# Keys and values of an attention kernel from unsplit fp32 products, two token blocks side by side

## The chip, the cores and the metric

The kernel runs on one core of one Trainium2 chip, in one launch. The metric is the device time of that core in microseconds (us), lower is better; the time of a kernel is the median of its runs. In the tables of the profile PE is the matrix engine (TensorE), PEld its weight loads, DVE the vector engine, ACT the scalar engine, POOL the GpSimd engine, and SP the engine whose queue issues all of this kernel's DMAs.

## The reference

Two independent blocks are computed and joined on the last axis. The first is attention with one key/value head, the second a two-dimensional Fourier mixing.

```python
q = (x @ wq)  # 2048 x 1024 tokens, 32 heads of 32
k = x @ wk    # 2048 x 32, shared by all heads
v = x @ wv    # 2048 x 32
p = softmax(q k^T * 32 ** -0.5)
a = (p @ v, heads joined) @ wo
b = dft_seq_re @ (xb @ dft_hid_re.T) - dft_seq_im @ (xb @ dft_hid_im.T)
out = concatenate([a, b], axis=-1)
```

## The kernel before, in words

**Split products.** All large products are made of three: each operand is rounded to `float32r` (the high part, `rh` or `mh`) and the rounding error is kept (the low part, `rl` or `ml`), and a product is high by high, low by high and high by low. A chunk of 128 of the contracted axis is thus three PE products of 512 columns (`product`, line 345). A `Group` (line 77) is one tile of 128 x 512 outputs with its chunks, 24 products for 8 chunks. Its right side is moving data in tiles of 128 x 512, its left side two tiles of four weight chunks. What a group does with its result is its `post`.

**Filling.** The groups stand in one list, and `take(n)` (line 351) issues the next n products of that list; `pos["fill"]` counts them. `pump` (line 290) runs ahead of that count: two lines (`RL` for right sides, `ML` for left sides, lines 256 and 257) load, convert to a high part and convert to a low part so many products before the need. While `pos["fill"]` is under `START`, ACT makes the high parts and DVE the low ones; later POOL makes both (`cast`, line 173, and `lo`, line 243). All DMAs go through SP in program order, and a DMA whose buffer isn't free holds up all that stand behind it.

**The start.** The tokens are four blocks of 512 (`b` = 0 to 3), each 8 chunks of `xT`. In the list stand first four key/value groups (`kv_group`, line 415: x chunks against the joined `wkv` of 64 columns, so that only 64 of 128 output rows are in use), for blocks 1, 2, 3 and 0 in that order of loading, then two query groups of block 0; `START` is these six groups, 144 products. `kv_post` (line 393) copies keys and values out, puts high, high and low parts of the keys into rows 0 to 95 of `kst` (one written by DVE, two moved by DMA), and transposes the values into `v` by four PE transposes, 20 products later. The first 26 tiles of x are loaded at once into buffers that are needed later for other things (line 718 on: `pp`, name `p`, and `hp`, names `h0` to `h7`). After the first six groups `open_unit(0)` (line 585) loads the scaled queries of the first unit, which a query group's post has stored to DRAM in a high part `qh` and a low part `ql`, into `qst`. Then come 66 more products of query groups.

**Units.** A unit is four heads of one query block, 32 units in all. `score_step` (line 699) makes the scores of one tile, `DVE` takes the row maximum, `ACT` the exponential with its row sum. 44 score steps run ahead, each with `take(7)`. In the main loop (line 752) one step is a score step, an `expo` (two products and an exponential of 128 x 1024 on ACT), every eighth step a `pv` (16 plain fp32 products of 32 output columns, four of them side by side in the array), and as many products of the list as `goal` (line 741) spreads evenly over 1024 steps. The logarithms of a unit's row sums, tile `mt`, go into `qst` by DMA in `lse_4` (line 646), four steps before the first `expo` of the unit. The list after the query groups is the Fourier part and then the output product; the last groups are written out by hand (line 768 on), and each copies its result through a tile of the pool `op` (line 131) to the output.

**Pools that the change touches.** `op` holds the staging tiles of results: two of `qh`, one of `ql` (line 425). `yp` (line 130) holds six tiles `y0`, `qsp` three tiles `qst`, `onp` one `ov`.

Of the kernel before, what the change touches and what calls it, by code (L numbers as in the profile page):

```python
# [8 lines left out]
F32 = mybir.dt.float32  # L9
F32R = mybir.dt.float32r  # L10
AF = mybir.ActivationFunctionType
# [5 lines left out]
P = 128  # L17
# [3 lines left out]
DH = 32  # L21
W = 512
NG = 8
NQ = 4
NC = 16
ND = D // P
# [61 lines left out]
def tile_kernel(ctx: ExitStack, tc, xT, wq, wkv, wo, xbT, wT, cT, out):  # L88
    nc = tc.nc
    te = Ordered(tc, nc.tensor)  # L90
    act = Ordered(tc, nc.scalar)
    dve = Ordered(tc, nc.vector)
    gp = Ordered(tc, nc.gpsimd)
    sp = Ordered(tc, nc.sync)
    scale = float(DH) ** -0.5

    def pool(stack, name, bufs, **kw):
        kw.setdefault("reuse_waits", "tile")
        return stack.enter_context(tc.tile_pool(name=name, bufs=bufs, **kw))
# [12 lines left out]
    keep = pool(ctx, "keep", 1)  # L112
    ident = keep.tile([P, P], F32, name="ident")
    make_identity(nc, ident)
    kst = keep.tile([P, S], F32R, name="kst")
    dve.memset(kst[96:P, :].bitcast(F32), 0.0)
    dve.memset(kst[96:98, :].bitcast(F32), 1.0)
    v = keep.tile([P, NC, DH], F32, name="v")

    ps_s = pool(ctx, "ps_s", 2, space=PSUM)  # L120
    ps_t = pool(ctx, "ps_t", 1, space=PSUM)
# [6 lines left out]
    rp = pool(ctx, "rp", NR, side="right")  # L128
    mp = pool(ctx, "mp", NM, side="right")
    yp = pool(ctx, "yp", NY, side="right")  # L130
    op = pool(ctx, "op", 2, side="right")
    hp = pool(ctx, "hp", 1, side="right")

    def move(q, to, of):
        q.dma_start(to.bitcast(F32), of.bitcast(F32))


    class Line:
# [32 lines left out]
    pos = {"fill": 0, "s": 0}  # L171
# [84 lines left out]
    RL = Line(NR0, NR, (40, 40, 14, 8), load_r, comb, hi_r, lo)  # L256
    ML = Line(NM0, NM, (52, 36, 27, 21), load_m, comb, hi_m, lo)
# [87 lines left out]
    def product(g, ps, j):  # L345
        c, w = divmod(j, 3)
        l, r = g.left[c // 4], g.right[c]
        a = (l.lo if w == 2 else l.hi)[:, c % 4]
        te.matmul(ps[:g.rows], a, r.lo if w == 1 else r.hi, start=j == 0, stop=j == g.n - 1)

    def take(n):
        for _ in range(n):
            if cur["group"] >= len(groups):
                return
            g = groups[cur["group"]]
            j = pos["fill"] - g.at
            if j == 0:
                cur["ps"] = bank("psb", True)
            if j % 3 == 0:
                RL.force(g.right[j // 3])  # L360
            if j % 12 == 0:
                ML.force(g.left[j // 12])
            product(g, cur["ps"], j)
            pos["fill"] += 1
            if j == g.n - 1:
                cur["group"] += 1
                assert all(hasattr(it, "done") for it in g.ys)
                g.post(cur["ps"])
                cur["at"] += 1
                used[cur["bank"]] = cur["at"]  # L370
                cur["bank"] = None
                if g.ys:
                    at(pos["fill"] + 2 * BEHIND, lambda n=len(g.ys): yused.__setitem__(0, yused[0] + n))
            pump()
            run_later()
# [14 lines left out]
    def x_set(b):  # L390
        return [Item([(lambda c=c: xT[b, c], 1)]) for c in range(ND)]

    def kv_post(b):
        cols = slice(b * W, (b + 1) * W)

        def post(ps):
            kv = yp.tile([P, W], F32, name="y0")[:2 * DH]
            act.activation(kv, ps[:2 * DH], AF.Copy)
            dve.tensor_copy(kst[0:DH, cols], kv[0:DH])
            kl = yp.tile([P, W], F32, name="y0")[:DH].bitcast(F32R)  # L400
            dve.tensor_sub(kl, kv[0:DH], kst[0:DH, cols].bitcast(F32))
            move(sp, kst[DH:2 * DH, cols], kst[0:DH, cols])
            move(sp, kst[2 * DH:3 * DH, cols], kl)

            def v_out():
                pv = ps_s.tile([P, 2 * W], F32, name="pss")[:, :W].rearrange("p (a b) -> p a b", a=4)
                for j in range(4):
                    te.transpose(pv[:, j, :2 * DH], kv[:, j * P:(j + 1) * P], ident[:2 * DH, :2 * DH])
                dve.tensor_copy(v[:, b * 4:(b + 1) * 4, :], pv[:, :, DH:2 * DH])
            at(pos["fill"] + 20, v_out)  # L410
        return post

    wkv_items = [Item([(lambda q=q: wkv[:, q * 4:(q + 1) * 4, :], 1)]) for q in range(2)]

    def kv_group(b, xs):
        return Group(wkv_items, xs, kv_post(b), rows=2 * DH)

    ready = set()

    def q_group(b, g, xs):  # L420
        left = [Item([(lambda q=q: wq[g, :, q * 4:(q + 1) * 4, :], 1)]) for q in range(2)]

        def post(ps):
            qh = op.tile([P, W], F32R, name="qh")
            ql = op.tile([P, W], F32R, name="ql", bufs=1)
            if pos["fill"] <= START:
                act.activation(qh, ps, AF.Copy, scale=scale)
            else:
                dve.tensor_scalar_mul(qh, ps, scale)
            dve.scalar_tensor_tensor(ql, ps, scale, qh.bitcast(F32), op0=ALU.mult, op1=ALU.subtract)  # L430
            store(qh_d[b][g], qh)
            store(ql_d[b][g], ql, ("q", b, g))
        return Group(left, xs, post)
# [123 lines left out]

    def x_groups(b, kv, q):  # L560
        xs = x_set(b)
        return ([kv_group(b, xs)] if kv else []) + ([q_group(b, g, xs) for g in range(NG)] if q else [])

    first = x_groups(0, True, True)
    start = x_groups(1, True, False) + x_groups(2, True, False) + x_groups(3, True, False) + first[:2]
    START = 24 * len(start)
    rest = first[2:] + x_groups(1, False, True) + x_groups(2, False, True) + x_groups(3, False, True)
    rest += list(stage1()) + list(stage2())
    w1, w0 = wo_set(1), wo_set(0)
    rest += [o_group(b, t, e, ws) for e, ws in ((1, w1), (0, w0)) for b in range(NQ - 1) for t in range(4)]  # L570
# [144 lines left out]
    TURN = 6  # L715
    LSE = {1: (lse_1,), 2: (lse_1b,), 4: (lse_2,), 8: (lse_4,)}

    room = [(lambda t=t, k=k: t[:, k]) for t in [pp.tile([P, 2, W], F32, name="p") for _ in range(9)] for k in range(2)]
    room += [(lambda t=t: t) for t in [hp.tile([P, W], F32, name=f"h{k}") for k in range(8)]]
    for n, (it, to) in enumerate(zip(RL.items, room)):  # L720
        it.t = [to()]
        sp.dma_start(it.t[0], it.srcs[0][0]())
        if n == 1:
            ML.pump()
    pump()
    take(START)
    open_unit(0)
    take(66)
    for s in range(SU + LEAD):
        score_step(s)  # L730
        take(7)
# [20 lines left out]
    for n in range(total):  # L752
        u, r = divmod(n, SU)
# [41 lines left out]
    for t, g in enumerate(last[4:]):  # L795
        ps = ps_b[t % 2].tile([P, W], F32, name="psb")
# [41 lines left out]
```

## Time and profile before

| | us |
|---|---|
| median of 3 runs (2790.85 to 2792.5) | 2790.86 |
| the profiled execution, whole | 2791.25 |
| its span in the profile | 2789.3 |
| PE busy in the span | 2763.8 |
| ACT busy | 2181.4 |
| POOL busy | 1651.0 |
| DVE busy | 1624.4 |

The profiled execution's own time is 1.95 us over its span, and 0.39 us over the median. A row of the timeline reads: start, duration, engine, line, operation, output <- inputs, shape, count, and in brackets the idle time of that engine ahead of the row with what ended it. Line 66 is that of a helper through which every instruction goes, so rows are told apart by the names of their tiles. A PE row of one product lasts longer than the step to the next product, because products overlap; the step from start to start is what counts. A plain fp32 product stands as two PE rows in the profile, a product of `float32r` parts as one.

### The profile page before, as it was taken

To read this page: it belongs to the slowest core of one execution; us is meant where nothing else is said; L and a number is where in the kernel's file an instruction comes from. 1 tells how busy PE (TensorE), PEld (TensorE's weight loads), DVE (VectorE), ACT (ScalarE), POOL (GpSimd) and SP (SyncE) were. 2 spreads that over 40 slices of the span, in tenths; PEclk is the share of its full clock that TensorE was granted. 3 is DMA by queue.
4 is the path that set the end of the run, shared out by engine and by line. 5 is a ranking of instruction groups with operands and counts; after the bars stand their busy time and mean duration, and the time that the engine had idled before them with its cause. 6 is when DMAs were issued, how large, how long until landed. Compare 5 with 4: busy or idle time off the path is not lost.

```text
span 2789.3 us, 40153 instructions
## 1 busy us (share of the span) xinstructions
PE 2763.8 (99%) x13904; PEld 1932.7 (69%) x13904; DVE 1624.4 (58%) x1864; ACT 2181.4 (78%) x3151; POOL 1651.0 (59%) x1622
## 2 busy tenths in 40 slices
PE   8999999999999999999999999999999999999999
PEld 5876767667666767666676767667676767676666
DVE  6766666666676665555555655555565555555411
ACT  4578888888788888888888888878888888888740
POOL 3755534665535538767686567798887885640110
PEclk9999999999999999999999999999999999999999
DMA  7544325766576554545453454555564552554455
GB/s 253 197 140 129 110 103 174 242 213 203 189 237 212 171 175 156 162 144 153 143 189 104 129 167 139 160 198 162 163 193 150 167 160 80 159 163 140 126 166 173
DMA packets 304203, 459.87 MB, mean 165 GB/s; under 512 B 32128, under 2 KB 97152, under 8 KB 304000
## 3 DMA queue, kind: packets, MB, share of 16 engines
q1 hardware_dynamic: 304000, 457.30, 51.6%
q8 instruction: 110, 1.80, 0.3%
q14 instruction: 93, 0.76, 0.1%
HBM read 351.54 MB, written 104.60 MB: 164 GB/s over the span
## 4 chain that ended last, share of the span: by engine, by line
PE 96%; DMA 1%; DVE 1%; ACT 1%; issue 0%; POOL 0%; SPq 0%; ACTq 0%; POOLq 0%; DVEq 0%
PE psb L66 61%; PE pss L66 18%; PE pst L66 17%; DMA p<-in_xT_dram 0%; DVE nm L66 0%; ACT pss L66 0%; SPq L66 0%; DVE rl L66 0%; ACT p L66 0%; DMA r<-s 0%; ACT rh L66 0%; DMA qst<-mt 0%; DMA ql<-ql 0%; DMA r<-in_xT_dram 0%; POOL ml L66 0%
## 5 line engine op out<-in xcount | busy, mean ns | idle before, releaser
L66 DVE TENSOR_REDUCE nm<-pss 128x1 f32<-128x1024 f32 x1024 | 1252.7, 1223 | 591.2 <-PE pss L66 590.3
L66 ACT ACTIVATE p<-pst 128x1024 f32<-128x1024 f32 x1024 | 1052.2, 1028 | 463.8 <-PE pst L66 461.3
L66 ACT ACTIVATE pss<-pss,nm 128x1024 f32<-128x1024 f32 x1024 | 1112.9, 1087 | 67.3 <-DVE nm L66 65.9
L66 PE MATMUL psb<-rh,mh 128*128 128x512 f32 (+1 forms) x1852 | 730.4, 394 | 9.7 <-ACT rh L66 8.3
L66 PE MATMUL psb<-rh,ml 128*128 128x512 f32 (+1 forms) x1852 | 730.1, 394 | 2.2 <-POOL ml L66 2.2
L66 PE MATMUL psb<-rl,mh 128*128 128x512 f32 (+1 forms) x1852 | 728.5, 393 | 0.3 <-DVE rl L66 0.3
L66 PE MATMUL pss<-kst,qst 128*128 128x512 f32 x2048 | 657.1, 402 | 1.3 <-ACT pss L66 1.2
L66 PE MATMUL pst<-qst,kst 128*128 128x512 f32 x2048 | 649.5, 398 | 4.4 <-DMA qst<-mt 3.6
L66 PEld LDWEIGHTS pss<-kst,qst 128*128 128x128 f32 x2048 | 372.2, 188 | 184.7 <-issue 102.3
L66 POOL TENSOR_TENSOR ml<-m,mh 128x512 fp32r<-128x512 f32 x340 | 438.8, 1291 | 48.2 <-ACT mh L66 40.4
L66 PE MATMUL psb<-p,v 128*32 128x512 f32 x4096 | 466.3, 596 | 0.0
L66 PEld LDWEIGHTS pst<-qst,kst 128*128 128x128 f32 x2048 | 377.4, 188 | 112.2 <-ACT p L66 20.8
L66 PEld LDWEIGHTS psb<-rh,mh 128*128 128x128 f32 (+1 forms) x1852 | 346.7, 187 | 95.9 <-ACT rh L66 9.0
L66 PEld LDWEIGHTS psb<-rh,ml 128*128 128x128 f32 (+1 forms) x1852 | 346.6, 187 | 86.7 <-POOL ml L66 3.5
L66 PEld LDWEIGHTS psb<-rl,mh 128*128 128x128 f32 (+1 forms) x1852 | 346.7, 187 | 84.5 <-DVE rl L66 1.4
L66 PEld LDWEIGHTS psb<-p,v 128*32 128x32 f32 x4096 | 120.0, 109 | 276.6 <-issue 265.6
L66 POOL CAST mh<-m 128x512 fp32r<-128x512 f32 x339 | 208.1, 614 | 166.0 <-PE psb L66 145.3
L66 POOL TENSOR_TENSOR r<-r,r 128x512 f32<-128x512 f32 x112 | 144.4, 1289 | 271.6 <-DMA r<-s 135.2
L66 POOL CAST rh<-r 128x512 fp32r<-128x512 f32 x214 | 131.5, 614 | 262.0 <-PE psb L66 144.9
L66 POOL TENSOR_TENSOR rl<-r,rh 128x512 fp32r<-128x512 f32 x214 | 276.2, 1291 | 3.9
L66 POOL TENSOR_TENSOR m<-m,m 128x512 f32<-128x512 f32 x192 | 247.9, 1291 | 28.7 <-DMA m<-in_xbT_dram 20.6
L66 DVE TENSOR_TENSOR ov<-ov,psb 128x512 f32<-128x512 f32 x96 | 66.0, 688 | 272.0 <-PE psb L66 272.0
(68 smaller groups left out, 929.5 us busy)
## 6 DMA issues: line engine op xcount, KB each, us to landing
m<-in_cT_dram SPq DMA_DIRECT2D x384, 256.0 KB, 3.7
r<-s SPq DMA_DIRECT2D x192, 256.0 KB, 4.3
y<-y SPq DMA_DIRECT2D x96, 256.0 KB, 4.6
r<-in_wT_dram SPq DMA_DIRECT2D x80, 256.0 KB, 3.7
m<-in_xbT_dram SPq DMA_DIRECT2D x80, 256.0 KB, 4.2
y<-u SPq DMA_DIRECT2D x80, 256.0 KB, 2.8
m<-in_wq_dram SPq DMA_DIRECT2D x64, 256.0 KB, 3.0
qst<-qh SPq DMA_DIRECT2D x64, 256.0 KB, 5.5
```

What stands on the lines that cost most here:

```text
L66: return lambda *a, **k: self.tc.keep_in_program_order(f(*a, **k))
```

## The change

Keys and values leave the list. `kv_pair` makes them for two blocks at once from x and `wkv` as they were loaded, in plain fp32: block one's 64 output rows in rows 0 to 63 of one PSUM tile, block two's in rows 64 to 127. It then splits the keys on DVE and moves all three parts by DMA. All 32 tiles of x are loaded at the start, the last six into two tiles of `qst`; those of blocks 0 and 1 are also what the query groups of these blocks convert, while blocks 2 and 3 are still loaded once more for their query groups later. Three products of zeros (the tile `v`, cleared first) are issued ahead of the first group. `START` falls from 144 to 48. The 66 products ahead of the first score become 24. Low parts of queries go into the ring `y0` of six, and `op` has three `qh`.

```diff
+    v = keep.tile([P, NC, DH], F32, name="v")
+    dve.memset(v, 0.0)
     dve.memset(kst[96:P, :].bitcast(F32), 0.0)
     dve.memset(kst[96:98, :].bitcast(F32), 1.0)
-    v = keep.tile([P, NC, DH], F32, name="v")
...
-    op = pool(ctx, "op", 2, side="right")
+    op = pool(ctx, "op", 3, side="right")
...
+    def kv_pair(blocks, xs):
+        ps = ps_s.tile([P, 2 * W], F32, name="pss")[:, :W]
+        for c in range(ND):
+            for n, x in enumerate(xs):
+                te.matmul(ps[n * 2 * DH:(n + 1) * 2 * DH], wkv_t[:, c * 2 * DH:(c + 1) * 2 * DH], x[c], start=c == 0, stop=c == ND - 1)
+        kv = yp.tile([P, W], F32, name="y0")
+        act.activation(kv, ps, AF.Copy)
+        kh = op.tile([P, W], F32R, name="qh")
+        dve.tensor_copy(kh, ps)
+        kl = yp.tile([P, W], F32, name="y0").bitcast(F32R)
+        dve.tensor_sub(kl, ps, kh.bitcast(F32))
+        for n, b in enumerate(blocks):
+            rows = slice(n * 2 * DH, n * 2 * DH + DH)
+            for r, part in enumerate((kh, kh, kl)):
+                move(sp, kst[r * DH:(r + 1) * DH, b * W:(b + 1) * W], part[rows])
+        def v_out():
+            pv = ps_t.tile([P, 2, W], F32, name="pst")[:, 0].rearrange("p (a b) -> p a b", a=4)
+            for j in range(4):
+                te.transpose(pv[:, j], kv[:, j * P:(j + 1) * P], ident)
+            for n, b in enumerate(blocks):
+                dve.tensor_copy(v[:, b * 4:(b + 1) * 4, :], pv[:, :, (2 * n + 1) * DH:(2 * n + 2) * DH])
+        at(pos["fill"] + 20, v_out)
...
-            ql = op.tile([P, W], F32R, name="ql", bufs=1)
+            ql = yp.tile([P, W], F32, name="y0").bitcast(F32R)
...
+    sets = [x_set(b) for b in range(NQ)]
+    start = [q_group(0, g, sets[0]) for g in range(2)]
...
+    zeros = v[:, :, :].rearrange("p a b -> p (a b)")
+    for _ in range(3):
+        te.matmul(ps_t.tile([P, 2, W], F32, name="pst")[:, 0], zeros[:, :P], zeros, start=True, stop=True)
...
+    load_x(0)
+    for it in sets[0]:
+        RL.force(it)
+    wkv_t = onp.tile([P, W], F32, name="ov")
+    sp.dma_start(wkv_t, wkv.rearrange("p a b -> p (a b)"))
+    load_x(1)
+    for it in start[1].left:
+        ML.force(it)
     pump()
-    take(START)
+    load_x(2)
+    load_x(3)
+    take(24)
+    kv_pair((0, 1), xs[:2])
+    take(24)
     open_unit(0)
-    take(66)
+    kv_pair((2, 3), xs[2:])
+    take(24)
```

What this makes of the order on two engines is shown at three places. In the rows, names carry the number of the buffer, and what stands in brackets is what the instruction waits for. First, the start of PE's row, before:

```order
L66 MATMUL psb_457<-rh_449,mh_417 64x512 [waits Activation_49]
L66 MATMUL psb_457<-rl_450,mh_417 64x512 [waits DVE_49]
L66 MATMUL psb_457<-rh_449,ml_418 64x512
L66 MATMUL psb_457<-rh_452,mh_417 64x512 [waits Activation_49]
L66 MATMUL psb_457<-rl_453,mh_417 64x512 [waits DVE_49]
L66 MATMUL psb_457<-rh_452,ml_418 64x512
```

and with the change, where `pst` is the PSUM tile of the zero products and `psb_512` that of the first query group:

```order
L66 MATMUL pst_395<-v_282 128x512 [waits DVE_49]
L66 MATMUL pst_397<-v_282 128x512 [waits PE_49]
L66 MATMUL pst_399<-v_282 128x512 [waits PE_49]
L66 MATMUL psb_512<-rh_440,mh_425 128x512 [waits Activation_49]
L66 MATMUL psb_512<-rl_441,mh_425 128x512 [waits DVE_49]
L66 MATMUL psb_512<-rh_440,ml_426 128x512
```

The first list product is now one of 128 output rows and of the queries, and each chunk of x still waits for ACT and then DVE to convert it. Second, PE at the passage from one group to the next. Before, from the second key/value group (`psb_559`) to the third (`psb_637`):

```order
L66 MATMUL psb_559<-rl_519,mh_420 64x512 [waits DVE_49]
L66 MATMUL psb_559<-rh_518,ml_421 64x512
L66 MATMUL psb_637<-rh_525,mh_417 64x512
L66 MATMUL psb_637<-rl_526,mh_417 64x512 [waits DVE_49]
L66 MATMUL psb_637<-rh_525,ml_418 64x512
```

With the change, from the first query group to the first pair; `p_401` to `p_408` are the tiles of x, two chunks each (401 to 404 block 0, 405 to 408 block 1), and `ov_472` holds `wkv`:

```order
L66 MATMUL psb_512<-rh_468,mh_428 128x512 [waits Activation_49]
L66 MATMUL psb_512<-rl_469,mh_428 128x512 [waits DVE_49]
L66 MATMUL psb_512<-rh_468,ml_429 128x512
L66 MATMUL pss_554<-p_401,ov_472 64x512 [waits DMAHW2_49,DMAHW0_49]
L66 MATMUL pss_554<-p_405,ov_472 64x512 [waits DMAHW3_49]
L66 MATMUL pss_554<-p_401,ov_472 64x512
L66 MATMUL pss_554<-p_405,ov_472 64x512 [waits DMAHW4_49]
L66 MATMUL pss_554<-p_402,ov_472 64x512
```

The pair alternates between the two blocks chunk by chunk, 16 products in all, and these wait for DMAs alone; before, every one of the 96 key/value products stood behind conversions. Third, SP between the loads of x and the first unit's queries, before:

```order
L66 DMA kst_281<-kst_281 32x512
L66 DMA kst_281<-y0_760 32x512
L66 DMA m0_774<-in_wq_dram 128x512
L66 DMA r0_792<-in_xT_dram 128x512
L66 DMA m0_797<-in_wq_dram 128x512
L66 DMA qh_0_0_57<-qh_813 128x512
L66 DMA ql_0_0_89<-ql_814 128x512
L66 DMA qst_819<-qh_0_0_57 32x4x512
L66 DMA qst_819<-ql_0_0_89 32x4x512
```

and with the change (`m0` are weights of queries, `qst_637` is the tile of the first unit, `qh_573` and `y0_575` are the keys' parts of blocks 0 and 1):

```order
L66 DMA kst_281<-qh_573 32x512 x2
L66 DMA kst_281<-y0_575 32x512
L66 DMA m0_593<-in_wq_dram 128x512
L66 DMA m0_615<-in_wq_dram 128x512
L66 DMA qh_0_1_58<-qh_631 128x512
L66 DMA ql_0_1_90<-y0_632 128x512
L66 DMA qst_637<-qh_0_0_57 32x4x512
L66 DMA qst_637<-ql_0_0_89 32x4x512
```

The loads of the first unit's `qst` now stand behind the stores of the second query group (`qh_0_1`, `ql_0_1`) too; before, only those of the first (`qh_0_0`, `ql_0_0`) stood ahead of them.

More of the change, by code (lines that the diff above doesn't have):

```diff
@@ L391, in x_set @@
         return [Item([(lambda c=c: xT[b, c], 1)]) for c in range(ND)]
[L393 to L411, printed above, removed]
@@ L413, in tile_kernel @@
-    wkv_items = [Item([(lambda q=q: wkv[:, q * 4:(q + 1) * 4, :], 1)]) for q in range(2)]
-    def kv_group(b, xs):
-        return Group(wkv_items, xs, kv_post(b), rows=2 * DH)
+    def kv_pair(blocks, xs):
[20 more added lines that the diff above has]
+        at(pos["fill"] + 20, v_out)
@@ L554, in o_group @@
         return Group([o_left(b, t, q) for q in range(2)], ws, post)
[L560 to L565, printed above, removed]
+    sets = [x_set(b) for b in range(NQ)]
+    start = [q_group(0, g, sets[0]) for g in range(2)]
     START = 24 * len(start)
-    rest = first[2:] + x_groups(1, False, True) + x_groups(2, False, True) + x_groups(3, False, True)
+    rest = [q_group(b, g, sets[b]) for b in range(NQ) for g in range(0 if b else 2, NG)]
     rest += list(stage1()) + list(stage2())
@@ L716, in tile_kernel, with load_x @@
     LSE = {1: (lse_1,), 2: (lse_1b,), 4: (lse_2,), 8: (lse_4,)}
[L718 to L724, printed above, removed]
-    pump()
-    take(START)
+    zeros = v[:, :, :].rearrange("p a b -> p (a b)")
+    for _ in range(3):
+        te.matmul(ps_t.tile([P, 2, W], F32, name="pst")[:, 0], zeros[:, :P], zeros, start=True, stop=True)
+    room = [t[:, k] for t in [pp.tile([P, 2, W], F32, name="p") for _ in range(9)] for k in range(2)]
+    room += [hp.tile([P, W], F32, name=f"h{k}") for k in range(8)]
+    room += [t[:, k].bitcast(F32) for t in [qsp.tile([P, 4, W], F32R, name="qst") for _ in range(2)] for k in range(4)]
+    xs = [[room[b * ND + c] for c in range(ND)] for b in range(NQ)]
+    def load_x(b):
+        for c in range(ND):
+            sp.dma_start(xs[b][c], xT[b, c])
+            if b < 2:
+                sets[b][c].t = [xs[b][c]]
+            if b == 0 and c == 0:
+                ML.pump()
+    load_x(0)
[6 more added lines that the diff above has]
+        ML.force(it)
+    pump()
+    load_x(2)
[3 more added lines that the diff above has]
+    take(24)
     open_unit(0)
-    take(66)
+    kv_pair((2, 3), xs[2:])
+    take(24)
     for s in range(SU + LEAD):
```

## The prediction, made before the change was run

> **What bounds the kernel now.** I read the engines' busy time first, then the chain that ended last, then the time by stage (columns: stretch, its length, then busy time and instructions of PE, PEld, DVE, ACT, POOL, then the granted clock, the DMA share and GB/s).
>
> ```profile
> PE 2763.8 (99%) x13904; PEld 1932.7 (69%) x13904; DVE 1624.4 (58%) x1864; ACT 2181.4 (78%) x3151; POOL 1651.0 (59%) x1622
> PE 96%; DMA 1%; DVE 1%; ACT 1%; issue 0%; POOL 0%; SPq 0%; ACTq 0%; POOLq 0%; DVEq 0%
> ```
>
> ```profile
> 0.00:59.70 59.70, 49.49 (x202) 32.81 (x203) 38.30 (x59) 28.51 (x47) 14.62 (x20) 0.97 0.77 255
> 59.70:150.00 90.30, 88.03 (x379) 70.44 (x378) 66.24 (x76) 49.19 (x82) 69.41 (x76) 1.00 0.56 189
> 150.00:2735.00 2585.00, 2577.99 (x13116) 1791.32 (x13118) 1511.17 (x1717) 2103.67 (x3023) 1563.21 (x1524) 1.00 0.51 162
> 2735.00:2789.30 54.30, 48.26 (x216) 38.18 (x208) 8.72 (x13) 0.00 (x0) 3.73 (x4) 0.98 0.55 166
> ```
>
> PE carries the time nearly everywhere: from 150 to 2735 us it is idle for 7 us in all. So an instruction taken off PE there, or put there, counts at PE's own pace. The exception is the start: of the first 59.7 us PE is idle for 10.2. That is the stretch that the change rewrites, so I work out when it ends with the change, and correct for the products that are then still to do. The marks of that stretch on PE:
>
> ```profile
> 7.14 0.69 PE L66 MATMUL psb<-rh,mh 128*64 128x512 f32 x1 [7.14 <-ACT rh L66]
> 10.91 0.63 PE L66 MATMUL psb<-rh,ml 128*64 128x512 f32 x1
> 11.34 0.63 PE L66 MATMUL psb<-rh,mh 128*64 128x512 f32 x1
> 12.51 0.39 PE L66 MATMUL psb<-rh,mh 128*64 128x512 f32 x1
> 12.73 0.39 PE L66 MATMUL psb<-rl,mh 128*64 128x512 f32 x1
> 33.12 0.44 PE L66 MATMUL psb<-rh,mh 128*64 128x512 f32 x1 [1.17 <-ACT rh L66]
> 35.70 0.46 PE L66 MATMUL pss<-ident,y 64*128 64x64 f32 x4 [0.71 <-ACT y L66]
> 53.83 0.39 PE L66 MATMUL psb<-rl,mh 128*128 128x512 f32 x1
> ...
> 58.81 0.39 PE L66 MATMUL psb<-rh,ml 128*128 128x512 f32 x1
> ...
> 59.73 0.62 PE L66 MATMUL pss<-kst,qst 128*128 128x512 f32 x2
> ```
>
> Products begin at 7.14 and step by 0.43 us at first (10.91 to 11.34), by half of that from 12.5 on; undisturbed, the step is 0.2265 us (22 products from 53.83 to 58.81). There are waits in between, as at 33.12 and 35.70. The first scores stand at 59.73, with 96 key/value products and 48 + 66 = 114 query products done. With the change they come after two pairs and 72 query products, so 42 products more (42 x 0.2265 = **9.5 us**) remain for the full-pace part.
>
> **The change, step by step.**
>
> *First query group.* Ahead of PE stand conversions on ACT and DVE.
>
> ```profile
> 1.23 1.76 DVE L66 MEMSET kst<- 32x2048 f32 x1 [1.23 <-PEq L828]
> 3.48 1.76 DVE L66 MEMSET kst<- 2x2048 f32 x1 [0.48 <-DVE kst L66]
> 7.12 12.13 DVE L66 TENSOR_TENSOR rl<-p,rh 128x512 fp32r<-128x512 f32 x18
> ```
>
> ```profile
> 6.47 12.05 ACT L66 ACTIVATE rh<-p 128x512 fp32r<-128x512 f32 x18
> ```
>
> DVE's two clearings end at 5.24. The new one of `v` has a quarter of the columns, about 0.44 us more, so 5.7. Then DVE makes two `ml` and eight `rl` at 12.13 / 18 = 0.67: 5.7 + 6.8 = 12.5, and two products later the group ends, at **13.0**. ACT converts as fast (18 in 12.05) and starts ahead of DVE, and PE at 0.2265 x 3 = 0.68 a chunk keeps step. This holds if PE has its full pace by then. The three zero products can begin at 1.7 us. One fp32 product takes as long as four split ones (next paragraph), 4 x 0.43 = 1.7 us at the slow pace, so the three end at 6.9, where the first converted chunk comes anyway: nothing by themselves. In the profile the pace doubled 5 us after the first product (7.14 to between 11.8 and 12.5). If zeros do the same, the query group runs at full pace from its start; if they don't, some 10 products cost 0.2 us more, 2.0 us. I take 0, since PE works through those 5 us either way; the bounds are 0 and +2.0.
>
> *The pairs.* No row shows two fp32 products of 64 columns. The nearest is `pv`, 16 fp32 products of 32 columns, four side by side:
>
> ```profile
> 1002.64 3.64 PE L66 MATMUL psb<-p,v 128*32 128x512 f32 x32
> ```
>
> 3.64 us for four such sets is 0.91 a set, four times 0.2265. Side by side two halves of 64 columns cost the same 0.91 a chunk, a pair 8 x 0.91 = 7.3 us. One after the other it is twice that, 14.6. I take 7.3, the row that it is like; the other end costs 14.6 more over both pairs and is a rival below. The split products of 64 columns before don't tell, since they all went to the same rows, one after another. [...]
>
> Do the pairs wait for x? The DMAs run at their limit then (share 1.05, 393 GB/s):
>
> ```profile
> 10.00:20.00 10.00, 10.00 (x39) 5.49 (x37) 9.18 (x14) 9.27 (x16) 0.00 (x0) 1.00 1.05 393
> ```
>
> ```profile
> 5.63 0.93 ACT L66 ACTIVATE mh<-m 128x256 fp32r<-128x256 f32 x2 [3.61 <-DMA m<-in_wkv_dram]
> ```
>
> The first 786 KB had landed by 5.63, which is three loads with the change; each further 256 KB takes 0.67. So the 10th load (last x of block 0) is there at 10.3, the 19th (block 1) at 16.3, the 38th (block 3) at 29.0. Pair one needs block 1's chunk k at 13.0 + 0.91 k and it lands at 11.6 + 0.67 k, so it isn't held up. It ends at **20.3**. Loading x once thus matters by what ACT and DVE are spared: 24 tiles need no conversion at the start.
>
> *Query group two, pair two, query group three.* 24 products are 5.4 us. The four transposes in the midst are shown before:
>
> ```profile
> 42.99 0.39 PE L66 MATMUL psb<-rl,mh 128*128 128x512 f32 x1
> 43.31 0.46 PE L66 MATMUL pss<-ident,y 64*128 64x64 f32 x4
> 43.70 0.50 PE L66 MATMUL psb<-rh,ml 128*128 128x512 f32 x1
> ```
>
> 0.71 in place of 0.23, so 0.5 more: **26.2**. Pair two: 33.5 (its last chunk is wanted at 32.6 and landed at 29.0, a cover of 3.6 us). Group three: 33.5 + 5.9 = **39.4**. Its second weights are the 39th load (29.7), converted by ACT and DVE by 31.5, while PE wants them at 36.2.
>
> *The first scores.* The loads of `qst` stand behind the second query group's low part. ACT gets to that group only after the 40th load (30.4) and three conversions, DVE follows, so SP issues the loads at about 33.5 to 35.
>
> ```profile
> DMA to landing us min/median/max: 3.0/3.5/4.2
> ```
>
> They land at 38.5 to 39.2, just ahead of 39.4; I take no wait, 1 us if it is worse. Twelve moves of keys in place of eight lie beside products: the last six can be issued from 35 and land some 5 us later, and the second score step, which wants them, is at 41.5. So the start ends at 39.4, with the 42 products at 48.9, in place of 59.73: **-10.8**.
>
> *Staging.* DVE waits for the single `ql` and PE for DVE; at the end DVE waits for `op`:
>
> ```profile
> 64.28 0.69 DVE L66 SCALAR_TENSOR_TENSOR ql<-psb,qh 128x512 fp32r<-128x512 f32 x1 [1.80 <-DMA ql<-ql]
> ...
> 68.16 1.22 DVE L66 TENSOR_REDUCE nm<-pss 128x1 f32<-128x1024 f32 x1 [0.92 <-PE pss L66]
> ...
> 2761.84 0.69 DVE L66 COPY qh<-pss 128x512 f32<-128x512 f32 x1 [0.64 <-DMA out_dram<-qh]
> ```
>
> ```profile
> 67.39 0.73 PE L66 MATMUL pss<-kst,qst 128*128 128x512 f32 x2 [1.25 <-ACT pss L66]
> ...
> 2762.59 0.50 PE L66 MATMUL pss<-rh,oh 128*128 128x512 f32 x1 [1.42 <-DVE qh L66]
> ```
>
> With a ring of six the first goes, **-1.25**, since the row maximum behind `ql` is late next, and DVE has 0.92 us idle ahead of the following one (68.16). With a third `qh` DVE's third copy starts 0.64 earlier, and PE's wait falls from 1.42 to 0.8: **-0.64**.
>
> Sum: 10.8 + 1.25 + 0.64 = 12.7 us less than the profiled execution's 2791.25, which is 2778.6. That execution is 0.39 over the median of 2790.86, so against the median **2778.2**.
>
> **The rivals.**
>
> *The halves run one after the other.* For it: no row shows 64 columns side by side. Against it: 32 columns do. Price +14.6, and block 3 is no later: 2792.8, within 0.2% of before. Chance 0.11.
>
> *The gain of the start is eaten at unit starts, and the kernel is slower.* A unit's first `expo` needs `mt`, and its DMA stands on SP behind loads into buffers that POOL has yet to read.
>
> ```profile
> 1847.35 1.14 SPq L66 DMA_DIRECT2D qst<-mt  x2
> ```
>
> ```profile
> 1852.40 1.19 PE L66 MATMUL pst<-qst,kst 128*128 128x512 f32 x2 [3.60 <-DMA qst<-mt]
> ```
>
> ```profile
> 1852.00:1854.00 2.00, 1.60 (x4) 1.34 (x5) 0.00 (x0) 0.38 (x1) 0.35 (x2) 0.54 0.52 178
> 1848.00:1852.00 4.00, 0.80 (x4) 0.32 (x2) 1.22 (x1) 1.34 (x3) 4.00 (x4) 1.00 0.84 270
> ```
>
> POOL was busy all of the 4 us ahead, PE waited 3.6 us, and the clock behind it shows 0.54, so some 3.4 us at half pace, 1.7 more: 5.3 us a time, once in 32 units. The 42 products shift the list against the units, by 13 products there, half a group. That moves the stall to another unit, removes it or doubles it. None makes 2773, two 2783.5. From four more stalls on (4 x 5.3 = 21.2 against 12.7) the kernel is slower by over 0.2%: 2799. Against it: 31 units had none. Chance of one more or one fewer 0.35 within the forecast, of four more 0.06.
>
> *The change doesn't bring full pace and cover at the start* (zeros without effect, +2.0; `qst` late, +1; loads slower than 0.67, which eats the 3.6 us of cover and then counts): 2782 to 2787. Chance 0.15.
>
> **How the numbers follow.** The forecast with one stall fewer or more (2772 to 2784) has 0.64, the weak start 0.15, the halves in turn 0.11, the slower case 0.06, and a gain beyond 20 us 0.04. Leaving out no more than 0.2 gives 2770 to 2789. What a measurement of this kernel can tell from no change is about 0.2%, 5.6 us, so 2785.3 to 2796.4 is the same. Faster: 0.64 + 0.04 + most of the weak start, 0.78. Same: the halves in turn and the rest of it, 0.14. Slower: 0.08, the stalls and some halves in turn on a weak start.
>
> **What would show it.** The first score at 39 to 40 us in the new timeline, with the pairs as two blocks of about 7.3 us, and no row of PE over 0.5 us idle between 7 and 60. A pair of 14 us would prove the first rival. A clock row under 1 after 8 us would show that zeros don't count. More than one wait for `mt`, with a clock row near 0.5 behind it, would be the second. A first score at 39 with a total over 2786 and no such wait would prove that the 42 products cost more later than 0.2265 each, and the forecast wrong at its base.

## The result, and the profile after

The changed kernel takes **2774.7 us** (median of 4 runs, 2771.11 to 2776.12) against 2790.86 of the kernel before (4 runs, 2788.97 to 2792.5). The ratio is 0.9936, with a 95% interval of 0.9924 to 0.9948. The forecast was 2778.2. The profiled execution took 2775.04 (span 2773.1, before 2789.3), so the span fell by 16.2 us where 12.7 were forecast.

First a correction to the text ahead of the result, since a term of the sum hangs on it: before, `START` is 120 products, not 144. `first[:2]` is the key/value group of block 0 and one query group, so five groups stand ahead of `open_unit(0)`, and 24 + 66 = 90 query products are done at the first scores, not 114. PE's rows say so: of the 202 before 59.70 us, 16 are transposes and 96 belong to keys and values, which leaves 90.

The page of the changed kernel: busy time, then the chain that ended last.

```profile
PE 2756.9 (99%) x13870; PEld 1924.6 (69%) x13870; DVE 1606.3 (58%) x1836; ACT 2169.8 (78%) x3126; POOL 1648.2 (59%) x1618
PE 95%; DMA 2%; POOL 1%; DVE 1%; issue 1%; SPq 1%; ACT 0%; POOLq 0%; ACTq 0%
```

Its time by stage, cut at the first scores as it was for the kernel before (stretch, length, busy time and instructions of PE, PEld, DVE, ACT, POOL, granted clock, DMA share, GB/s):

```profile
0.00:42.05 42.05, 37.58 (x150) 19.80 (x151) 20.26 (x31) 13.47 (x22) 9.30 (x14) 1.00 0.95 324
42.05:133.00 90.95, 90.80 (x385) 73.08 (x386) 67.67 (x76) 49.66 (x84) 67.23 (x73) 0.98 0.57 180
133.00:2719.00 2586.00, 2579.99 (x13125) 1793.48 (x13127) 1509.67 (x1716) 2106.64 (x3021) 1567.90 (x1528) 1.00 0.52 162
2719.00:2773.10 54.10, 48.49 (x216) 38.19 (x208) 8.73 (x13) 0.00 (x0) 3.75 (x4) 1.00 0.56 168
```

The start is 17.7 us shorter (59.73 to 42.05) with 202 - 150 = 52 fewer PE rows, and PE is idle there for 4.5 us in place of 10.2. The marks of it on PE, in the same view as before:

```profile
1.46 5.39 PE L66 MATMUL pst<-v 128*128 128x512 f32 x6 [1.46 <-DVE v L66]
6.93 0.49 PE L66 MATMUL psb<-rh,mh 128*128 128x512 f32 x1
7.89 0.50 PE L66 MATMUL psb<-rl,mh 128*128 128x512 f32 x1 [0.46 <-DVE rl L66]
8.22 0.39 PE L66 MATMUL psb<-rh,ml 128*128 128x512 f32 x1
8.45 0.39 PE L66 MATMUL psb<-rh,mh 128*128 128x512 f32 x1
...
13.32 7.09 PE L66 MATMUL pss<-p,ov 128*64 128x512 f32 x32
20.34 0.50 PE L66 MATMUL psb<-rh,mh 128*128 128x512 f32 x1
...
26.46 0.64 PE L66 MATMUL pss<-p,ov 128*64 128x512 f32 x1
...
33.48 0.50 PE L66 MATMUL psb<-rh,mh 128*128 128x512 f32 x1
...
39.31 0.39 PE L66 MATMUL psb<-rh,ml 128*128 128x512 f32 x1
42.05 0.70 PE L66 MATMUL pss<-kst,qst 128*128 128x512 f32 x2 [2.35 <-DMA kst<-qh]
```

Every mark up to 33.48 stands within 0.3 us of the forecast: the first group ends at 13.2 (forecast 13.0), the pair is one block of 7.09 (7.3), the second group begins at 20.34 (20.3), the second pair at 26.46 (26.2), the third group at 33.48 (33.5). Products step by 0.23 from 8.2 us on, and the trace's clock record has full clock from 5.65. But the last product of the start begins at 39.31, and the first scores only at 42.05, behind a wait of 2.35. The bracket names a part of the keys, but experiment e5 shows that PE waits for the loads of `qst`. SP issued those loads, and what stands just ahead of them, here:

```profile
32.70 0.99 SPq L66 DMA_DIRECT2D m<-in_wq_dram  x2
33.78 0.39 SPq L66 DMA_DIRECT2D qh<-qh  x1
34.35 0.33 SPq L66 DMA_DIRECT2D ql<-y  x1
34.72 0.49 SPq L66 DMA_DIRECT2D qst<-qh  x1
35.27 0.88 SPq L66 DMA_DIRECT2D qst<-ql  x1
36.19 0.46 SPq L66 DMA_DIRECT2D qst<-qh  x1
```

and this is how long they took, from the answer on the tile `qst`:

```profile
DMA to landing us min/median/max: 4.9/5.5/5.7
```

So they are issued 1.2 us later than forecast and take 5.5 us, not 3.5; the last lands at 36.19 + 5.7 = 41.9. Two weight loads and two stores of 256 KB each are issued in the 2 us ahead of them, and in e5, where they stand ahead of these four, they take 3.3 to 4.5. The lateness at issue comes from ACT, which converts the third group's weights ahead of the second group's result. That order was forecast, but with the first of these weights there at 29.7; in ACT's timeline their load ends a wait of 10.29 only at 31.36:

```profile
31.36 0.63 ACT L66 ACTIVATE mh<-m 128x512 fp32r<-128x512 f32 x1 [10.29 <-DMA m<-in_wq_dram]
...
32.94 0.58 ACT L66 ACTIVATE qh<-psb 128x512 fp32r<-128x512 f32 x1
```

Cut at the first scores, at the first `expo` on ACT and at the last `pv` of the loop, the two profiled executions compare like this:

| stretch | before | after | difference |
|---|---|---|---|
| start to first scores | 59.73 | 42.05 | -17.7 |
| first scores to first `expo` | 96.8 | 95.9 | -0.9 |
| first `expo` to last `pv` | 2556.1 | 2558.9 | +2.8 |
| the rest | 76.66 | 76.23 | -0.4 |
| sum | 2789.3 | 2773.1 | -16.2 |

The +2.8 are 18 query products more in the loop (4926 in place of 4908; 18 x 0.2265 = 4.1) less 1.4 of waits, which are read at 1700 to 2200 us. There PE waited 3.6 for `mt` and 2.2 for `ml` before, 5.8 in all; after, one row holds all of it. The rows for `ml`, before and after:

```profile
PE psb L66 <- POOL ml L66: 2.2, 3, 1.0
...
PE psb L66 <- POOL ml L66: 4.4, 4, 1.8
```

One more thing lies in these spans. Behind the wait for the first scores the clock is at half, 0.50 from 43.20 to 46.61 in the trace's clock record. In a view of 4 us around that:

```profile
43.00:47.00 4.00, 4.00 (x12) 3.08 (x12) 1.86 (x2) 1.21 (x2) 2.74 (x4) 0.57 0.87 273
```

The same kernel in another execution (r1) has a wait of 2.60 at this place and no such spell:

```profile
43.00:47.00 4.00, 4.00 (x19) 3.22 (x18) 2.45 (x2) 1.83 (x3) 2.82 (x4) 1.00 0.94 260
```

12 products in 4 us against 19. The spell at half clock lasts 3.41 us and costs half of it, 1.7; the 7 products that are missing in the row are 7 x 0.2265 = 1.6. The shown execution of before has two (36.3 and 1852 us), that of after two (43.2 and 1855.7), r1 none, and its span is 2769.5, 3.6 below that of after. So two spells are most of the difference between two executions of one kernel, and spans are compared below with their spells counted.

### The profile page after: what moved, and what is told of

Same layout as the page of the kernel before. It is cut to its first block, busy times and chain, and to the rows that moved or that the text cites. A ratio compares the mean times of both kernels' runs of the same rounds, so it can differ in the third digit from the quotient of the medians.

```text
span 2773.1 us, 39970 instructions
## 1 busy us (share of the span) xinstructions
PE 2756.9 (99%) x13870; PEld 1924.6 (69%) x13870; DVE 1606.3 (58%) x1836; ACT 2169.8 (78%) x3126; POOL 1648.2 (59%) x1618
## 4 chain that ended last, share of the span: by engine, by line
PE 95%; DMA 2%; POOL 1%; DVE 1%; issue 1%; SPq 1%; ACT 0%; POOLq 0%; ACTq 0%
PE psb L66 60%; PE pss L66 18%; PE pst L66 17%; DMA r<-s 1%; DMA p<-in_xT_dram 1%; SPq L66 1%; POOL ml L66 0%; DMA m<-in_wq_dram 0%; DVE qh L66 0%; DMA h<-in_xT_dram 0%; DVE y L66 0%; ACT p L66 0%; ACT pss L66 0%; DVE nm L66 0%; POOL mh L66 0%
## 5 line engine op out<-in xcount | busy, mean ns | idle before, releaser
L66 PE MATMUL psb<-rh,ml 128*128 128x512 f32 x1820 | 716.7, 394 | 4.4 <-POOL ml L66 4.4
L66 PE MATMUL psb<-rh,mh 128*128 128x512 f32 x1820 | 716.7, 394 | 0.5 <-DVE y L66 0.4
L66 PE MATMUL psb<-rl,mh 128*128 128x512 f32 x1820 | 714.6, 393 | 0.5 <-DVE rl L66 0.5
L66 PEld LDWEIGHTS psb<-rh,ml 128*128 128x128 f32 x1820 | 341.9, 188 | 86.1 <-POOL ml L66 6.1
L66 PEld LDWEIGHTS psb<-rh,mh 128*128 128x128 f32 x1820 | 341.8, 188 | 85.3 <-issue 1.2
L66 PEld LDWEIGHTS psb<-rl,mh 128*128 128x128 f32 x1820 | 341.8, 188 | 80.5 <-DVE rl L66 0.8
L66 POOL TENSOR_TENSOR rl<-r,rh 128x512 fp32r<-128x512 f32 x208 | 269.0, 1294 | 3.8
```

Source lines behind the costliest of these rows:

```text
L66: return lambda *a, **k: self.tc.keep_in_program_order(f(*a, **k))
```

## The experiments

The theory: PE's own work at the start is what the change saves, the pairs of 64 columns run side by side, and what is lost again is the wait for `qst` and 18 products in the loop. The rivals: the halves run in turn; the zeros bring the full pace that counts; the new staging makes the gain. Each ratio is against the kernel before on the same chip, with its 95% interval.

### e1: the halves one after the other

```diff
-        for c in range(ND):
-            for n, x in enumerate(xs):
+        for n, x in enumerate(xs):
+            for c in range(ND):
```

> The pair's 16 products are issued block by block instead of alternating, so that neighbours write the same rows. Theory, that the two halves run side by side in the array: a pair goes from the 7.1 us seen with the change to 16 x 0.86 = 13.8 us, both pairs cost 13.4 us more, and the kernel is near 2788 us. Rival, that plain fp32 products of 64 columns cost 0.43 us each in any order: the pairs stay at 7.1 us and the time at 2775.

Measured: 2781.12 (2780.52 to 2781.45), ratio 0.9959 (0.9944 to 0.9975). The pair and the first scores on PE:

```profile
13.54 12.29 PE L66 MATMUL pss<-p,ov 128*64 128x512 f32 x32
...
50.18 0.62 PE L66 MATMUL pss<-kst,qst 128*128 128x512 f32 x2
```

12.29 us in place of 7.09: the halves do run side by side in the changed kernel, and it is the order of issue that allows it. It isn't twice 7.09, and the reason is to be seen when the pair is cut in three (stretch, length, busy PE and rows of the pair that lie in it, clock, DMA share, GB/s):

```profile
13.54:18.60 5.06, 5.05 (x12) 1.00 1.05 387
18.60:20.50 1.90, 1.90 (x9) 1.00 1.06 389
20.50:26.00 5.50, 5.33 (x14) 1.00 1.05 387
```

A row about every 0.4 us at first and last (12 in 5.06, 14 in 5.50), but twice as many in the middle (9 in 1.90). At the passage from one half to the other rows of the second half run beside the last ones of the first, though they stand behind them in the program: five rows lie in 18.9 to 19.5 us, where rows of 0.59 us with a step of 0.43 give three. Both pairs cost 10.4 more, and the first scores come 8.1 later, not 10.4, since the wait of 2.35 is filled. Between executions without a clock spell the span is 9.4 longer (2778.9 against 2769.5 of r1).

### e2: no zero products

```diff
-    for _ in range(3):
-        te.matmul(ps_t.tile([P, 2, W], F32, name="pst")[:, 0], zeros[:, :P], zeros, start=True, stop=True)
```

> The three zero products are left out. Theory, that they do nothing but bring the full clock before the first query group: about 10 to 12 of its products step by 0.43 instead of 0.2265 us, the group ends 1 to 2 us later than at 13.3, and the kernel takes 1 to 2 us more. Rival, that DVE's conversions pace this group at 0.67 us a chunk at any clock: the group ends within 0.5 us of 13.3 and the time is the same.

Measured: 2772.82 (2772.07 to 2773.32), ratio 0.993 (0.9917 to 0.9942).

```profile
16.09 7.09 PE L66 MATMUL pss<-p,ov 128*64 128x512 f32 x32
...
42.32 0.62 PE L66 MATMUL pss<-kst,qst 128*128 128x512 f32 x2
```

With the zeros full pace comes earlier: the changed kernel's clock record has full clock from 5.65, and without them the step between products falls from 0.42 to 0.23 only at 13.24. The pair begins 2.8 us later. But the first scores come 0.3 later only, and without a wait. The wait of 2.35 for `qst` in the changed kernel had swallowed what the zeros had gained.

### e5: the loads of `qst` earlier

```diff
     kv_pair((0, 1), xs[:2])
-    take(24)
     open_unit(0)
+    take(24)
```

> The first unit's queries are asked for ahead of the second run of 24 products instead of behind it, so that their three loads stand on SP ahead of two weight loads and of the stores of the second query group. All products and their order on PE are those of the change. Theory, that PE's wait at the first scores (2.35 us, ended at 42.05, then 3.4 us at half clock) is for these three loads, issued at 34.7 to 36.6 and 5.5 us on their way: issued at about 32.5 they land by 39.5, the first scores stand at 39.6 to 40 and the kernel takes 2 to 4 us less than 2774.7, less what the second scores then wait for the moves of keys. Rival, that the wait is for a move of keys into kst, as the row of the profile names it: the first scores stay at 42 or later and the time is the same.

Measured: 2774.03 (2771.17 to 2774.5), ratio 0.9932 (0.992 to 0.9945). On SP:

```profile
32.32 0.45 SPq L66 DMA_DIRECT2D qst<-qh  x1
...
33.32 0.43 SPq L66 DMA_DIRECT2D qst<-qh  x1
...
DMA to landing us min/median/max: 3.3/3.7/4.5
```

on PE:

```profile
39.73 0.62 PE L66 MATMUL pss<-kst,qst 128*128 128x512 f32 x2
42.19 0.96 PE L66 MATMUL pss<-kst,qst 128*128 128x512 f32 x2 [0.21 <-PE psb L66]
```

The moves of keys keep their place in the order, the loads of `qst` go 2.4 us earlier and take 3.7 in place of 5.5, and the wait is gone. So PE waited for `qst`, and the bracket of the changed kernel named the wrong transfer. The gain isn't kept, though. Against r1 (neither has a clock spell) the first scores are 2.6 earlier (39.73 and 42.30), the first `expo` 1.9 (134.71 and 136.63), and the last `pv` 0.25 (2693.01 and 2693.26). In between, PE's waits for `ml` sum to 4.8 in place of 3.8, and a new one for `qst` adds 0.6. That is 1.6 of the 1.9, given back in a stretch where POOL, which makes `ml`, is what PE waits for.

### e4: the 18 products back ahead of the scores

```diff
     kv_pair((2, 3), xs[2:])
-    take(24)
+    take(42)
```

> The last of the three runs of query products ahead of the first scores has 42 instead of 24, which brings the count there to 90, as before the change. Theory, that PE waits at the first scores (2.35 us, and 3.4 us at half clock behind it) for DMAs that land at a time of their own, and that a product costs 0.2265 us wherever it stands: the 18 products take 4.1 us there and save 4.1 later, the wait and the slow clock go, and the kernel takes 4 us less, 2771. Rival, that the wait moves along with the products since the DMAs are issued behind them: no change.

Measured: 2773.59 (2772.85 to 2773.99), ratio 0.9932 (0.992 to 0.9945), 1.1 below the changed kernel. The first scores stand at 44.29 with no wait: 18 products (4.1 us) more for 2.2 us, as the wait is filled. Two waits of the kernel before are back: the one for `mt`, and one of 1.03 at 143 us, here at 126. The rows of before (143 us) and of e4:

```profile
143.29 0.47 PE L66 MATMUL psb<-rh,mh 128*128 128x512 f32 x1 [1.03 <-DVE ql L66]
...
126.29 0.47 PE L66 MATMUL psb<-rh,mh 128*128 128x512 f32 x1 [1.02 <-DVE y L66]
...
1834.97 0.70 PE L66 MATMUL pst<-qst,kst 128*128 128x512 f32 x2 [3.09 <-DMA qst<-mt]
```

The waits at 1700 to 2200 are 3.1 for `mt` and 2.4 for `ml`, 5.5 in all, against 4.4 in the changed kernel and 3.8 in r1. Where the list stands against the units decides which waits there are. Less the 1.7 of its one clock spell the span is 2770.4, against 2769.5 of r1: what the start gains is lost in these waits, and the 4 us of the theory aren't there.

### e3: the old staging in the changed kernel

```diff
-    op = pool(ctx, "op", 3, side="right")
+    op = pool(ctx, "op", 2, side="right")
...
-            ql = yp.tile([P, W], F32, name="y0").bitcast(F32R)
+            ql = op.tile([P, W], F32R, name="ql", bufs=1)
```

> Two qh and a single ql again, all else with the change. Theory, that the staging alone was worth 1.25 us behind the first scores and 0.64 us at the end: 1 to 2 us more, with DVE waiting for the DMA of ql and PE's wait for the copies of the end back at about 2.2 us in two times. Rival, that with the change's start these waits fall into time that is spare: less than 0.5 us more.

Measured: 2776.32 (2774.4 to 2776.6), ratio 0.994 (0.9927 to 0.9952), 1.6 above the changed kernel, with intervals that overlap.

```profile
139.84 0.73 PE L66 MATMUL pss<-kst,qst 128*128 128x512 f32 x2 [0.66 <-ACT pss L66]
...
2745.76 0.50 PE L66 MATMUL pss<-rh,oh 128*128 128x512 f32 x1 [1.41 <-DVE qh L66]
```

Both kinds of wait that the staging was to shorten are there with it: 1.41 at the end (0.78 after), and 0.66 in place of none behind the single `ql`, though at 140 us and not just behind the first scores, and half as long as before (1.25). Less the 1.7 of its one clock spell the span is 2771.0, 1.5 over that of r1.

### e7: the new staging alone, in the kernel before

```diff
-    op = pool(ctx, "op", 2, side="right")
+    op = pool(ctx, "op", 3, side="right")
...
-            ql = op.tile([P, W], F32R, name="ql", bufs=1)
+            ql = yp.tile([P, W], F32, name="y0").bitcast(F32R)
```

> The kernel before with only the staging of the change: three qh, and the low parts of queries in the ring y0 of six. Theory, that DVE's waits for the single ql made PE wait 1.25 us behind the first scores, and two qh 0.64 us at the end: 1.3 to 2 us less than before. Rival, that these waits are covered: within 0.5 us of before.

Measured: 2789.93 (2788.46 to 2792.57, 11 runs), ratio 0.9992 (0.9984 to 1.0001). The wait of 1.25 at 67 us is gone and the waits at the end are 0.78 and 0.78 in place of 0.78 and 1.42. The 1.03 at 143 us stays (1.0). The ratio leaves anything from a gain of 4.5 us to a loss of 0.3; the waits are what shows the mechanism.

### e8, r1 and r2: without zeros again

e8 is e5 without the zero products, r1 the changed kernel once more, r2 e2 once more.

> As e5_open_early, and without the three zero products. Theory, that zeros are worth the 2.8 us by which the first pair began later without them (16.1 against 13.3), and that this was hidden only since PE then waited for the first unit's queries: here the first scores come 2 to 3 us later than in e5_open_early and the kernel takes 1.5 to 3 us more than it. Rival, that the start is bound by DMAs whatever PE does: the two are within 0.7 us.

> The changed kernel once more, beside the same kernel without zeros on one chip, since without them the medians so far lay 1 to 2 us lower, against the theory of 2 us more. Theory, that zeros are worth nothing to the whole as long as PE waits for the first unit's queries: 2773 to 2775.5, level with r2_no_zeros within 1 us. Rival, that zeros cost 1 to 2 us somewhere: this one is slower than r2_no_zeros by that.

> The changed kernel without the three zero products, as e2_no_zeros. Theory: level with r1_after within 1 us, 2773 to 2775. Rival: 2772 to 2773, 1 to 2 us under r1_after.

| kernel | zeros | median (lowest to highest) | ratio | profiled span | spells in it |
|---|---|---|---|---|---|
| after | yes | 2774.7 (2771.11 to 2776.12) | 0.9936 (0.9924 to 0.9948) | 2773.1 | 2 |
| r1 | yes | 2775.23 (2771.45 to 2778.16) | 0.9942 (0.9929 to 0.9954) | 2769.5 | 0 |
| e2 | no | 2772.82 (2772.07 to 2773.32) | 0.993 (0.9917 to 0.9942) | 2771.3 | 0 |
| r2 | no | 2773.1 (2771.47 to 2773.61) | 0.9935 (0.9923 to 0.9948) | 2770.8 | 0 |
| e5, `qst` early | yes | 2774.03 (2771.17 to 2774.5) | 0.9932 (0.992 to 0.9945) | 2769.4 | 0 |
| e8, `qst` early | no | 2771.93 (2770.91 to 2774.04) | 0.9927 (0.9914 to 0.9941) | 2770.5 | 0 |

Two readings go apart. By the medians the kernels without zeros are 1.9 to 2.1 us faster, three times out of three. By the profiled executions without a spell they are 1.1 to 1.8 slower (e2 and r2 against r1, e8 against e5). With `qst` early, where nothing hides the zeros, they bring the first scores 1.7 us forward (39.73 against 41.41) and the first `expo` 1.1 (134.71 against 135.80). No profile shows a place where the zeros cost.

The granted clock, which the record has for every run, tells where the medians part. All 15 runs of e2, r2 and e8 show 1.0; of the 14 of after, r1 and e5 eight show 0.998 or 0.999. The other six have spans of 2769.2 to 2772.4, the 15 without zeros 2769.1 to 2772.2. So, as far as these runs tell, the medians with zeros are higher by time at reduced clock, not by products that take time. In the changed kernel the wait at the first scores, which e2 and r2 don't have, is followed by such time (the spell at 43.2); e5 has no such wait, and why two of its five runs lose clock isn't shown.

e8 has the lowest median of all versions, 2.8 under the changed kernel, but its interval overlaps the others.

### e9: the zeros alone, in the kernel before

```diff
+    v = keep.tile([P, NC, DH], F32, name="v")
+    dve.memset(v, 0.0)
     dve.memset(kst[96:P, :].bitcast(F32), 0.0)
...
+    zeros = v[:, :, :].rearrange("p a b -> p (a b)")
+    for _ in range(3):
+        te.matmul(ps_t.tile([P, 2, W], F32, name="pst")[:, 0], zeros[:, :P], zeros, start=True, stop=True)
```

> The kernel before with only the three zero products and the clearing of v ahead of everything. Theory, that they end by the time the first converted chunk comes and bring the full clock: the first 12 products, which step by 0.43 us before, step by 0.23 us or wait for DVE at 0.67 us a chunk, the first scores come 1 to 2 us earlier than 59.73, and the kernel takes 1 to 2 us less. Rival, that DVE and the later wait for x at 33 us swallow it: first scores at 59 to 60 and the same time within 0.5 us.

Measured: 2794.71 (2791.5 to 2799.58, 11 runs), ratio 1.001 (1.0001 to 1.0019).

```profile
1.46 5.39 PE L66 MATMUL pst<-v 128*128 128x512 f32 x6 [1.46 <-DVE v L66]
...
20.20 0.43 PE L66 MATMUL pss<-ident,y 64*128 64x64 f32 x4 [2.70 <-ACT y L66]
...
59.80 0.62 PE L66 MATMUL pss<-kst,qst 128*128 128x512 f32 x2
```

Products step by 0.23 from 7.64 in place of 12.51, and PE then waits for ACT (2.70 here, 0.48, 0.56 and 1.52 later). The first scores are at 59.80 against 59.73: the old start isn't helped by a faster PE. The median is 2.7 above that of the kernel before beside it (2792.01), and the granted clock is lower here too: 0.998 or less in 9 of 11 runs, in 8 of 21 of the kernel before.

### e10: `mt` earlier, in the kernel before

```diff
-    LSE = {1: (lse_1,), 2: (lse_1b,), 4: (lse_2,), 8: (lse_4,)}
+    LSE = {1: (lse_1,), 2: (lse_1b,), 4: (lse_2,), 7: (lse_4,)}
```

> The kernel before with the DMAs of a unit's mt one score step earlier, about 2.5 us. It tells what the waits between 1700 and 2200 us are, which differ from kernel to kernel. Theory, that PE waits there for the place of mt in SP's queue (3.6 us once, and 1.7 us of slow clock): that wait goes to about 1 us and the kernel takes 2 to 5 us less. Rival, that POOL is the bound in that stretch and the wait only changes its name: waits for POOL's ml take its place, all waits between 1700 and 2200 us still sum to 4 to 6 us, and the time is the same within 1.5 us.

Measured: 2788.74 (2783.94 to 2791.33, 11 runs), ratio 0.9989 (0.998 to 0.9998). At 1700 to 2200 us PE's waits are these:

```profile
PE psb L66 <- POOL ml L66: 3.1, 2, 2.1
```

The 3.6 for `mt` are gone, 0.9 of them come back as waits for `ml` (2.2 before). So 2.7 of the 5.8 us stay away, and the median is 3.3 below the 2792.01 of the kernel before, within the theory's 2 to 5 (the interval leaves 0.6 to 5.6): the wait didn't only change its name.

### e11: both waits taken away, with the zeros

e5 with the edit of e10. It was to settle whether the zeros cost by themselves or through clock spells.

> The changed kernel with open_unit(0) ahead of the second group's take and with the logarithms of a unit's row sums finished at key 7 instead of 8. What is open: kernels with the zero products have medians about 2 us above the same kernels without them, while their best executions are no slower. Theory of the clock windows: in the executions profiled so far the clock stands at half pace in windows of 3.41 us, each of which costs 1.7 us, and each begins a whole number of 3.41 us behind the moment at which full clock was first granted. The zeros cost nothing themselves (spans without such a window are 2769.5 and 2769.4 with zeros and 2770.5 to 2771.3 without), but move that grid against the waits of about 2 us. Then taking away the waits for qst and mt should leave fewer such windows: a span of 2767 to 2769.5 without one, the median at 2770 to 2772, and any window that is left on the grid, behind a wait for ml. Rival, the zeros cost time by themselves at a place not seen: the median stays at 2773 to 2775, as with open_unit alone.

Measured: 2773.34 (2771.55 to 2774.14), ratio 0.9931 (0.9917 to 0.9944), profiled span 2772.1 with one spell. No wait for `mt` is left, but the next one on SP's queue has come up:

```profile
1800.50 0.70 PE L66 MATMUL pss<-kst,qst 128*128 128x512 f32 x2 [1.87 <-DMA qst<-qh]
```

and behind it is the spell:

```profile
1801.00:1806.00 5.00, 5.00 (x16) 3.92 (x15) 2.39 (x3) 2.79 (x4) 4.40 (x5) 0.66 0.50 177
```

The median is in the rival's range (2773 to 2775) and above the theory's (2770 to 2772); the span less 1.7 is 2770.4, also above the theory's. The wait ahead of the spell is a new one, and whether the spell begins a whole number of 3.41 us behind the first full clock isn't shown by these views. So this theory isn't borne out as it stands: with two waits taken away a third came up. Nor does the run bear out the rival: three of its five runs show a clock of 1.0, with spans of 2769.8 to 2771.7, level with the kernels without zeros.

## Why the prediction was right, and where it was off

**What bounds the kernel: right.** PE is busy 99% in both, and outside the start PE's work and a few us of waits make the time.

**First group, pairs, second and third group: right**, to 0.3 us each. The halves side by side were the largest unknown, and the row of four `pv` sets in 3.64 us was the right one to go by: 7.09 measured for 7.3. In turn a pair takes 12.29 (e1), so the rival is out.

**The 42 products: the step that failed.** They are 18, as corrected above. The term "42 x 0.2265 = 9.5" should have been 4.1, so the gain was forecast 5.4 us too small. The error is one of counting groups in `first[:2]`, not of the profile.

**The first scores at 39.4: off by 2.65.** The products were done at 39.5, as forecast. "I take no wait, 1 us if it is worse" was wrong in the landing: 5.5 us in place of 3.5, from a row of the old start. In the new one four transfers of 256 KB are issued just ahead of these loads; where the loads stand ahead of those four, they take 3.7 (e5), near the row. The bound of 1 us was too small as well. A clock spell behind it adds 1.7 in this execution.

**The zeros at nothing: the number right, the reason not.** Without them the first pair begins 2.8 later in e2 and 1.9 in e8, so the bound of 2.0 was too small, and "PE works through those 5 us either way" isn't why they bring nothing: the wait for `qst` hides it (e2). The test by the clock row couldn't have told, since that row stands at 1.00 while products step by 0.43 at the start (e2, 6 to 13 us); the step tells.

**Staging -1.25 and -0.64: right in mechanism** (e3, e7). The wait of 1.03 at 143 us, not named in the prediction, is gone as well. e7 keeps it, so it isn't the staging's, and e4 has it again, so it goes with the 18 products.

**The stall for `mt`: moved, not multiplied.** The rival of four more stalls is out. The cost isn't a stall of 5.3 that is there or not, but 3.1 to 5.8 us of waits at 1700 to 2200 us in all kernels compared, for `mt`, for `ml` or both by how the list falls against the units. e10 shows that the part for `mt` can be taken away for the most part.

**The sum.** Forecast -12.7; 24 products fewer -5.4; the later scores +2.65; the clock spell behind them +1.7; the wait of 1.03 -1.0; waits in the loop -1.4. That makes -16.2, the measured fall of the span; the smaller differences of the other terms cancel. That the forecast is off by 3.5 us only is in part luck: two errors of opposite sign, 5.4 and 4.35, nearly met. Either alone would still have left the time within 2770 to 2789.

## What to carry to other kernels

Here 16 fp32 products of 64 output rows each that alternate between the two halves of the array took 7.09 us, and 12.29 issued in turn. Two such pairs, 2 x 7.09 us, stand for what took 96 x 0.2265 = 21.7 as split products, and they spare the conversions; in turn (2 x 12.29) they cost more than the split ones. When a start is rewritten around PE, count which transfers are issued just ahead of the first small loads before taking their landing from a row, since the last of them sets the end: with four such transfers it took 5.5 us here, without them 3.7. And before pricing what is saved, follow it to the next stretch that another engine bounds: 2.6 us saved at the start by e5 were 0.25 us at the end of the loop.

## What the runs showed of the hardware

- **Half clock behind waits of PE.** In the clock records of the two traces of before and after, the clock is 0.50 for 3.41 us four times, not counting the stretch in which a record ends: from 36.25 and 1852.14 us before, from 43.20 and 1855.67 after. In the 3.41 us ahead of these, PE is idle for 1.28, 3.35, 2.27 and 1.83 us. The spells begin 23.89 and 1839.78 us behind the first full clock (12.36) before, and 37.55 and 1850.02 behind it (5.65) after: 7, 539, 11 and 542 times 3.4133 us. What is behind this isn't shown. The length of a wait alone doesn't tell in these runs: 1.87 us in e11 and 2.35 in the changed kernel were followed by a spell, 2.60 in r1 wasn't.
- **Full pace came earlier with products of zeros ahead.** They begin at 1.46 us, and the clock record has full clock from 5.65; without them (e2) the first product begins at 7.58, and the step falls from 0.42 to 0.23 at 13.24.
- **Rows of the second column half ran beside earlier ones of the first** in e1, where the halves are issued in turn: five rows in 18.9 to 19.5 us, where a step of 0.43 gives three.
- **A bracket in the profile named the wrong transfer**: `kst<-qh` for the wait of 2.35 at 42.05 in the changed kernel, where moving the loads of `qst` alone, 2.4 us ahead, removed the wait (e5).
